# An H3 convolution and MLP stack on one core: a residual stream kept less its mean, and the second product's outputs in two 320-column banks

## The chip, the core and the metric

The kernel runs on one core of one Trainium2 chip. The metric is the device time of the whole kernel in microseconds, the median of three runs. The engines are TensorE (PE, matmuls; PEld, its weight loads), VectorE (DVE), ScalarE (ACT), GpSimd (POOL) and SyncE (SP, which issues nearly all transfers).

## The reference

Two identical layers act on a stream `x` of 2048 rows by 640 columns in float32. Each layer adds a convolution gated by the normalised stream and then a dense network:

```python
x = A_q
x = x + _A_ref(_layernorm(x, axis=-1), A_k, A_v, A_shift_k, A_ssm_k, A_ssm_D)
x = x + _B_ref(_layernorm(x, axis=-1), B_w1, B_w2)
x = x + _A_ref(_layernorm(x, axis=-1), A_k, A_v, A_shift_k, A_ssm_k, A_ssm_D)
x = x + _B_ref(_layernorm(x, axis=-1), B_w1, B_w2)
```

`_layernorm(x)` is `(x - m) / sqrt(v + 1e-5)` along the 640 columns. `_A_ref(q, k, v, ...)` computes `k_shift`, a causal convolution of `k` with 4 taps per column, multiplies it by `v`, convolves that along all 2048 rows with `ssm_k` (one filter per column, by FFT), adds `ssm_D` times the product, and returns `q * y`. The result `y` does not depend on `x`, so both layers use the same one. `_B_ref(x, w1, w2)` is `relu(x w1) w2`, with `w1` 640 by 1728 and `w2` 1728 by 640.

## The kernel before, in words

The 2048 rows are 8 chunks of two halves of 128 rows. `order` is the list of the dense network's passes ("mains"): chunks 0 and 1 go half by half through layer 0 and layer 1, then the chunks 2 to 7 both halves at once. Ahead of a chunk's first main, `conv_to` has its convolution worked out: `transform` (the short taps, the multiplication by `v`, cosine and sine transforms on TensorE) and `products` (a convolution over chunks in the transformed domain: multiplies and adds of 128x768 on VectorE, L559, L593, L596, L597, whose operands `Ax` and `Gx` are stored to memory and loaded back; then an inverse transform into `pq`, L619). The output is written as rows `ys` (L651, L652), stored as `Y` and loaded again as `y` before each layer's gate. For chunk 0 there is no store in between: `products` gates the stream itself (`direct`, L666, L667).

`prep` makes a main's input. `stats` computes the mean and the reciprocal deviation of each row: `negm` (L785, VectorE), a square with its sum (L788, ScalarE), a root, VectorE's reciprocal (L791), a few one-column refining steps on ScalarE (L796 to L800), and `xn`, the normalised stream (L810, ScalarE). The gate is `xn = y * xn` (L851) and `x = x + xn` with its row sums (L855), both on VectorE. Then `stats` runs once more and the result is split in a float16 high half (L884, ScalarE) and a low half (L885, VectorE), both transposed by transfers (L897). For the first halves the chain is another one (L840 to L869), and TensorE transposes the first of them (L904).

`main` multiplies with split weights: three matmuls for each product of high and low halves, but two where a low half is dropped. The first product (`mm1`, L1018 and L1020 in the first main, L1030 to L1033 in the others) goes to a bank `h` of up to 512 columns; ScalarE takes the relu as high half `hh` (L1086), VectorE the low half (L1087); the last group of 256 hidden columns has its own path (`tb`, `down`, `hb`, L1090 to L1101). The second product (`mm2`) has the hidden part as its stationary operand and writes 640 columns for each half:

```python
        o = lambda s, h: oc[:, s] if h else ob[s].t
        ds = (slice(0, H), slice(H, D)) if wino else (slice(0, 512), slice(512, D))
```

so the first 512 go to the bank `o0` or `o1` and the last 128 to a part of the bank `oc` (for the second main, of the bank `x`), which both halves share. The residual add (L1177) reads them in two instructions of 512 and 128 columns, with two partial sums that L1185 adds. The last three mains (`WINO`) use another scheme with 320-column banks (L957, with L1122 to L1143 behind it); this scheme's own arithmetic is the same before and after.

Weights are loaded once as float32. `norms` computes a power-of-two scale for each of the two weight matrices: TensorE multiplies each of the 28 weight tiles by itself into `pw` (L699), VectorE takes the diagonal's sum (`dg`, L704), TensorE adds over partitions (`pn`, L706), and a chain of one-column steps gives `wn`, `wnr`, `wpw` and `wsc` (L707 to L710). TensorE's 70 idle-time matmuls `spin` (L716) keep it running meanwhile. `wsplit` then splits each weight tile in a high half (L731, ScalarE) and a low half (L732, VectorE), of 128x640.

The order of every engine's instructions is written out by a planner. Each operation is given to it with an engine, a cost, what it reads and writes, and a priority (`CRIT`, `URGENT`, `SOON`, `FILL`, `BACK` and others). The planner simulates the engines by the costs, picks the best ready operation for each engine as it comes free, and starts an operation that opens a new buffer only when its ring has one. So a change in one operation's cost, buffer or priority can move others on any engine. The engines run their lists in order, waiting by semaphores.

Of the kernel before, what the change touches and what calls it, by code (L numbers as in the profile page):

```python
# [63 lines left out]
AADD, RADD = (), ()  # L64
# [11 lines left out]
class Tile:  # L76
    def __init__(self, ring, shape, dtype, name, stream=0):
        self.ring, self.shape, self.dtype, self.name, self.stream = ring, list(shape), dtype, name, stream
        self.t, self.left, self.writer, self.readers = None, 0, None, []
        if ring is not None:  # L80
            ring.lines.setdefault(stream, []).append(self)
# [4 lines left out]
    def r(self, pat, **kw):  # L86
        return self.t.rearrange(pat, **kw)

# [10 lines left out]
class Plan:  # L99
# [5 lines left out]
    def op(self, eng, cost, fn, reads=(), writes=(), prio=0, nbytes=0, late=0.0):  # L105
# [9 lines left out]
        for t in writes:  # L115
            if t.writer is not None:
                deps.add(t.writer)
            elif t.ring is not None and not t.left:
                o.new.append(t)
            deps.update(t.readers)  # L120
# [4 lines left out]
        o.tiles = list({id(t): t for t in (*reads, *writes)}.values())  # L125
# [8 lines left out]
    def order(self):  # L134
# [9 lines left out]
        def fits(o):  # L144
            at = {}
            for t in o.new:
                k = at.setdefault(t.ring, {})
# [14 lines left out]
        while n < len(self.ops):  # L162
# [27 lines left out]
            for e in engs:  # L190
# [17 lines left out]
                for t in best.new:  # L208
                    t.ring.free -= 1
                    t.ring.lines[t.stream].pop(0)  # L210
# [22 lines left out]
    def issue(self):  # L233
        out, end = self.order()
        for o in out:
            for t in o.new:
                t.t = t.ring.pool.tile(t.shape, t.dtype, tag=t.ring.tag, name=t.name, bufs=t.ring.bufs)
# [5 lines left out]
def tile_h3_mlp(ctx: ExitStack, tc: tile.TileContext, q, kT, vT, shk, hF, hR, dD, w1, w2, cM, cG, out):  # L243
# [65 lines left out]
    POOL.memset(c15.t, 1.5)  # L309
    shs = keep(const, [P, NDT, 4], "shs")  # L310
# [22 lines left out]
    def pieces(u, ap):  # L333
# [23 lines left out]
        "p0": (ps, "o0", 1, 1),  # L357
        "p1": (ps, "o1", 1, 1),
    }

    def transform(u):
        ring = ALT if u == [(0, 2), (0, 3)] else MAIN

        def R(k, shape, name):
            pl, tag, bufs, stream = ring[k]
# [184 lines left out]
    def products(u, at, gt, after):  # L550
# [98 lines left out]
        act(h, lambda: ACT.activation(qs.t, pq[:, 256 : 256 + h].rearrange("p (a b) -> p a b", a=n), AF.Copy), [pq], [qs], pr_)  # L649
        pp = lambda: pq[:, 0:h].rearrange("p (a b) -> p a b", a=n)  # L650
        dve(h, lambda: DVE.tensor_sub(yo(0), pp(), qs.t), [pq, qs], [dst[0]], pr_)  # L651
# [11 lines left out]
        if direct:  # L663
            xs, xns, sp0 = first[c]
            for s in range(2):
                dve(h, lambda s=s: DVE.tensor_mul(xns[s][:, cs], xns[s][:, cs], dst[s][:, cs]), [xns[s], dst[s]], [xns[s]], (CRIT, BACK)[s])  # L666
                dve(h, lambda s=s: DVE.scalar_tensor_tensor(xs[s][:, cs], xns[s][:, cs], 1.0, xs[s][:, cs], op0=ALU.mult, op1=ALU.add, accum_out=sp0[s][:, 0, t0 // 2 : t0 // 2 + 1]), [xns[s], xs[s]], [xs[s], sp0[s]], (CRIT, BACK)[s], 0.2)  # L667
# [14 lines left out]
    def norms():  # L682
        ones = T(cv, "u", 2, [P, P], "ones", stream=1)
        plan.op("POOL", 0.5, lambda: POOL.memset(ones.t, 1.0), [], [ones], SOON)
        out_ = []
        for k, e in ((0, 9), (1, 13)):
            pw2 = T(ps, *(("h", 2), ("oc", 1))[k], [P, 2, P], f"pw{k}", stream=1)
            for j in JS:
                for i in range(2):
# [5 lines left out]
                    def f(m=2 * j + i, t=t, pw2=pw2):  # L695
                        top = t.t.bitcast(BF16).rearrange("p (n two) -> p n two", two=2)[:, :, 1]
                        for d in range(NDT):
                            x = top[:, d * P : d * P + P]
                            PE.matmul(pw2[:, 0], x, x, start=(m == 0 and d == 0), stop=(m == 2 * JS[-1] + 1 and d == NDT - 1))  # L699
# [4 lines left out]
            dve(P, lambda jk=jk, pw2=pw2, s2=s2: DVE.scalar_tensor_tensor(jk.t, pw2[:, 0], 1.0, ident.t, op0=ALU.mult, op1=ALU.mult, accum_out=s2.t), [pw2, ident], [jk, s2], URGENT, 0.2)  # L704
            pn = T(ps, "x", 1, [P, 512], f"pn{k}", stream=1)
# [73 lines left out]
    def small(tag, name):  # L779
        return T(mlp, tag, 2, [P, 2], name)  # L780

    def stats(xs, sums, name, S, pr=0, fine=False):
        q_ = slice(S[0], S[-1] + 1)
        negm, ssq, sd, r, v, nmr = (small(k, k + name) for k in ("negm", "ssq", "std", "rstd", "var", "nmr"))
        dve(2, lambda: DVE.tensor_scalar(negm[:, q_], sums[:, q_], -1.0 / D, None, op0=ALU.mult), [sums], [negm], pr)  # L785
        for s in S:
# [13 lines left out]
            (0.19 * len(S), [r, negm], [nmr], lambda: [A(nmr[:, c], r[:, c], ident_, scale=negm[:, c]) for c in cols]),  # L800
        ]
        if fine:
            for cost, rd, wr, f in steps:
                act(0, f, rd, wr, pr, cost - 0.1)
        else:
            act(0, lambda: [f() for *_, f in steps], [ssq, sd, negm, heps, c15], [v, r, nmr], pr, sum(x[0] for x in steps))
# [20 lines left out]
    def add_sum(x, t, sums, s):  # L827
        plan.op("POOL", 1.1, lambda: POOL.dma_start(out=x.t, in_=t.t, accum_op=ALU.add), [x, t], [x], URGENT, 8 * D * P)
        if sums is not None:
            act(D, lambda: ACT.activation(t.t, x.t, AF.Copy, accum_out=sums[:, s : s + 1]), [x], [t, sums], URGENT, 0.1)  # L830

    def prep(a, layer, S, pr=0):
# [4 lines left out]
        if head:  # L837
            xs, _, sp0 = first[a]
# [3 lines left out]
        else:  # L842
# [6 lines left out]
            xns = stats(xs, sums, "A" + nm, S)  # L849
            for s in S:  # L850
                ew("ay", D, lambda e, s=s, xn=xns[s]: e.tensor_mul(xn.t, ys[s].t, xn.t), [ys[s], xns[s]], [xns[s]], URGENT)  # L851
                if (a, layer) in AADD:
                    add_sum(xs[s], xns[s], sums2, s)
                    continue
                dve(D, lambda s=s, xn=xns[s]: DVE.scalar_tensor_tensor(xs[s].t, xn.t, 1.0, xs[s].t, op0=ALU.mult, op1=ALU.add, accum_out=sums2[:, s : s + 1]), [xns[s], xs[s]], [xs[s], sums2], URGENT, 0.2)  # L855
# [24 lines left out]
        else:  # L880
            xns = stats(xs, sums2, "B" + nm, S, pr)
        for s in S if not head else ():
# [454 lines left out]
```

## Time and profile before

| what | before |
|---|---|
| runs | 858.65, 859.96, 864.69 us (median 859.96) |
| span of the profiled execution (no other time of it is given) | 858.4 us |
| instructions | 19,690 |
| TensorE matmuls busy | 843.4 us (98%) |
| VectorE busy | 743.1 us (87%) |
| ScalarE busy | 482.2 us (56%) |
| GpSimd busy | 46.5 us (5%) |
| transfers | 178.05 MB, mean 207 GB/s |

Busy time is an average over stages. The profile's page gives it for the whole span, the table by stretches for chosen windows; the list of waits names for each engine what it waited for, the groups of instructions show the mean time of one form, and the timeline shows each start. Matmuls overlap: a row of 0.38 us can be followed by the next after 0.22, so the spacing of starts says what a matmul costs.

### The profile page before, as it was taken

What the parts mean: (1) busy time and instruction counts of PE and PEld (TensorE: products, weight loads), DVE (VectorE), ACT (ScalarE), POOL (GpSimd) and SP (SyncE); (2) the same over time, 40 slices, a digit from 0 to 9 for tenths busy, and PEclk for the clock granted to TensorE, in tenths of its full rate; (3) what the DMA queues carried; (4) which work ended last, traced back from release to release, by engine and by line L of the source; (5) the groups of instructions that cost most, each with busy time, mean ns of one, the idle gap of its engine ahead of it and who ended that gap; (6) DMA issues with size and microseconds to landing.
All of it is one profiled execution on the core that took longest, in us unless ns stands there. A gap on an engine that the chain in (4) does not pass through costs nothing.

```text
span 858.4 us, 19690 instructions
## 1 busy us (share of the span) xinstructions
PE 843.4 (98%) x7808; PEld 663.1 (77%) x7808; DVE 743.1 (87%) x1367; ACT 482.2 (56%) x1121; POOL 46.5 (5%) x57
## 2 busy tenths in 40 slices
PE   8989999999999999999999999999999999999997
PEld 7867877777878777777777777878777777888886
DVE  7999999999889999999999999999897575645543
ACT  6597586455686375728448383835416275727331
POOL 2000000000011001101010000001000000000000
PEclk9999999999999999999999999999999999999999
DMA  9994968798999979889788988687985562110100
GB/s 325 391 296 150 270 192 287 213 340 281 310 260 284 325 192 270 201 255 252 197 245 243 223 236 168 184 189 241 266 272 200 135 216 31 44 20 2 43 20 32
DMA packets 133838, 178.05 MB, mean 207 GB/s; under 512 B 50545, under 2 KB 87153, under 8 KB 133746
## 3 DMA queue, kind: packets, MB, share of 16 engines
q1 hardware_dynamic: 125426, 166.31, 62.5%
q0 software_dynamic: 8320, 10.49, 8.1%
q8 instruction: 61, 1.00, 0.5%
q14 instruction: 31, 0.25, 0.1%
HBM read 122.03 MB, written 34.08 MB: 182 GB/s over the span
## 4 chain that ended last, share of the span: by engine, by line
PE 81%; DVE 10%; DMA 4%; ACT 3%; issue 2%; SPq 1%; DVEq 0%; ACTq 0%
PE h L1030 12%; PE h L1033 12%; PE h L1031 12%; PE o L1003 8%; PE o L1002 8%; PE o L1005 7%; PE o L957 7%; PE oc L1003 2%; PE oc L1002 2%; PE oc L1005 2%; DMA A<-at 1%; PE pq L619 1%; DVE pd L596 1%; PE hb L1030 1%; PE hb L1031 1%
## 5 line engine op out<-in xcount | busy, mean ns | idle before, releaser
L1030 PE MATMUL h<-xT,w 128*128 128x256 f16 (+1 forms) x1290 | 301.5, 252 | 0.7 <-DVE hh L1087 0.6
L1033 PE MATMUL h<-xT,w 128*128 128x256 f16 (+1 forms) x1290 | 301.3, 251 | 0.4 <-DVE w L732 0.4
L1031 PE MATMUL h<-xT,w 128*128 128x256 f16 (+1 forms) x1290 | 301.3, 251 | 0.0
L1031 PEld LDWEIGHTS <-w 128*128 128x128 f16 x1390 | 136.0, 98 | 11.2 <-issue 1.0
L1030 PEld LDWEIGHTS <-w 128*128 128x128 f16 x1390 | 135.9, 98 | 10.4 <-ACT w L737 0.2
L1003 PE MATMUL o<-w,hh 128*128 128x512 f16 x364 | 137.9, 379 | 0.4 <-DVE w L732 0.4
L1002 PE MATMUL o<-w,hh 128*128 128x512 f16 x364 | 138.1, 379 | 0.0
L1033 PEld LDWEIGHTS <-w 128*128 128x128 f16 x1290 | 126.2, 98 | 9.8 <-DVE w L732 0.6
L597 DVE TENSOR_TENSOR pacc<-pacc,pd 128x768 f32<-128x768 f32 x140 | 133.0, 950 | 0.5
L1003 PEld LDWEIGHTS <-hh 128*128 128x128 f16 x728 | 71.2, 98 | 45.8
L1002 PEld LDWEIGHTS <-hh 128*128 128x128 f16 x728 | 71.2, 98 | 44.6 <-issue 0.2
L1086 ACT ACTIVATE hh<-h 128x512 f16<-128x512 f32 (+1 forms) x103 | 50.4, 489 | 97.7 <-PE h L1033 94.4
L1005 PE MATMUL o<-w,hl 128*128 128x512 f16 x234 | 88.7, 379 | 0.0
L1003 PE MATMUL oc<-w,hh 128*128 128x128 f16 x364 | 79.7, 219 | 0.0
L1002 PE MATMUL oc<-w,hh 128*128 128x128 f16 x364 | 79.7, 219 | 0.0
L596 DVE TENSOR_TENSOR pd<-Ax,Gx 128x768 f32<-128x768 f32 x83 | 77.8, 951 | 0.9 <-DMA Gx<-G 0.8
L1005 PEld LDWEIGHTS <-hl 128*128 128x128 f16 x468 | 45.8, 98 | 27.6
L1005 PE MATMUL oc<-w,hl 128*128 128x128 f16 x234 | 51.2, 219 | 0.0
L394 ACT ACTIVATE tp<-kt,shs 128x256 f32<-128x256 f32 (+1 forms) x78 | 42.7, 574 | 13.0 <-DVE acc L431 10.8
L1087 DVE SCALAR_TENSOR_TENSOR hl<-h,hh 128x512 f16<-128x512 f32 x55 | 37.6, 685 | 11.0 <-ACT hh L1086 11.0
L596 DVE TENSOR_TENSOR pd<-at,Gx 128x768 f32<-128x768 f32 x46 | 43.2, 951 | 0.6 <-DMA Gx<-G 0.5
L412 POOL DMA_DIRECT2D gs<-hr x20 | 19.6, 980 | 387.5 <-DVE pacc L593 189.1
(232 smaller groups left out, 1666.6 us busy)
## 6 DMA issues: line engine op xcount, KB each, us to landing
Ax<-A SPq DMA_DIRECT2D x89, 384.0 KB, 4.5
Gx<-G SPq DMA_DIRECT2D x89, 384.0 KB, 4.1
G<-gt SPq DMA_DIRECT2D x30, 384.0 KB, 5.2
A<-at SPq DMA_DIRECT2D x30, 384.0 KB, 4.6
y<-Y SPq DMA_DIRECT2D x30, 320.0 KB, 4.7
ws<-in_w SPq DMA_DIRECT2D x28, 320.0 KB, 6.6
x<-in_q SPq DMA_DIRECT2D x16, 320.0 KB, 5.5
out_dram<-x SPq DMA_DIRECT2D x16, 320.0 KB, 4.0
```

Source lines behind the costliest of these rows:

```text
L394: ACT.activation(o[:, i : i + m], kview(i, m, j), AF.Copy, scale=shs[:, t, j : j + 1])
L596: ew(f"mac{j % POOLMOD}", 768, lambda e, pd=pd, av=av, gv=gv: e.tensor_mul(pd.t, av(), gv()), [ax, gx], [pd], pr_)
L597: dve(768, lambda i=i, pd=pd: DVE.tensor_add(acc[:, i], acc[:, i], pd.t), [acc, pd], [acc], pr_)
L957: PE.matmul(b[:, c : c + w], x, y[:, z : z + w], start=done[i] == 1, stop=done[i] == total[i])
L1002: PE.matmul(z, hh[:, c], wh[:, d], start=(j == JS[0] and i == 0 and (h == 0 or s == S[0])), stop=False)
L1003: PE.matmul(z, hh[:, c], wl[:, d], start=False, stop=end and tail)
L1005: PE.matmul(z, hl[:, c], wh[:, d], start=False, stop=end)
L1030: PE.matmul(p[:, z], wh, xv(t, 0), start=b, stop=False)
L1031: PE.matmul(p[:, z], wh, xv(t, 1), start=False, stop=tail and e)
L1033: PE.matmul(p[:, z], wl, xv(t, 0), start=False, stop=e)
L1086: act(2 * R, lambda p=p, hh=hh: ACT.activation(hh.t, p.t, AF.Relu), [p], [hh], URGENT)
L1087: dve(2 * R, lambda p=p, hh=hh, hl=hl: DVE.scalar_tensor_tensor(hl.t, p.t, 0.0, hh.t, op0=ALU.max, op1=ALU.subtract), [p, hh], [hl], URGENT)
```

## The change

*The gate.* Before, `x + y * ((x - m) r)` took one ScalarE and two VectorE instructions. After, ScalarE computes `q = 1 + r * y` and one VectorE instruction `x = (x - m) * q` with its row sums. This is the old result less `m`, so the stream is kept less its mean: `MEAN` holds the means of each half (`keepm`, one-column ScalarE steps), and in layer 1 ScalarE adds them back to `x` (16 instructions of 128x640). For chunk 0, `products` forms `q` from the two parts of `pq` directly, and the rows that are stored for the next layer (`qs`, `yd`) get the priority `BACK`.

*Negative means* (`negm` in `stats`) move from VectorE to ScalarE.

*The banks.* A second product's half has two banks of 320 columns (`banks`, tags `oA` and `oB`), and one VectorE instruction over both reads them for the residual add. The sums of `norms` (`pw1`, `pn`), the transposes of the first half and one of the transforms use the same banks. `o0`, `o1`, `oc` and `x` are gone, as is a path that was off (`AADD`, `RADD`).

The core of the diff:

```diff
-        dve(2, lambda: DVE.tensor_scalar(negm[:, q_], sums[:, q_], -1.0 / D, None, op0=ALU.mult), [sums], [negm], pr)
+        act(2, lambda: ACT.activation(negm[:, q_], sums[:, q_], AF.Copy, scale=-1.0 / D), [sums], [negm], pr, 0.1)
...
-            xns = stats(xs, sums, "A" + nm, S)
+            negm, r, _ = stats(xs, sums, "A" + nm, S, gate_=True)
             for s in S:
-                ew("ay", D, lambda e, s=s, xn=xns[s]: e.tensor_mul(xn.t, ys[s].t, xn.t), [ys[s], xns[s]], [xns[s]], URGENT)
...
-                dve(D, lambda s=s, xn=xns[s]: DVE.scalar_tensor_tensor(xs[s].t, xn.t, 1.0, xs[s].t, op0=ALU.mult, op1=ALU.add, accum_out=sums2[:, s : s + 1]), [xns[s], xs[s]], [xs[s], sums2], URGENT, 0.2)
+                qx = T(mlp, "xn", 2, [P, D], f"q{nm}{s}")
+                act(D, lambda s=s, qx=qx: ACT.activation(qx.t, ys[s].t, AF.Identity, scale=r[:, s : s + 1], bias=one.t), [ys[s], r, one], [qx], URGENT, 0.09)
+                dve(D, lambda s=s, qx=qx: DVE.scalar_tensor_tensor(xs[s].t, xs[s].t, negm[:, s : s + 1], qx.t, op0=ALU.add, op1=ALU.mult, accum_out=sums2[:, s : s + 1]), [qx, xs[s], negm], [xs[s], sums2], URGENT, 0.2)
+            keepm(a, negm, S)
...
             xns = stats(xs, sums2, "B" + nm, S, pr)
+            if layer:
+                for s in S:
+                    act(D, lambda s=s: ACT.activation(xs[s].t, xs[s].t, AF.Identity, bias=MEAN[a][:, s : s + 1]), [xs[s], MEAN[a]], [xs[s]], URGENT, 0.1)
...
+    def banks(tag, name, stream=0, shape=(512,), dtype=F32):
+        x = T(ps, tag, 1, [P, 2, *shape], name, dtype, stream)
+        return [Bank(x, k) for k in range(2)]
...
+        pw1, pn = banks("oB", "pw1", 2)
...
-            pn = T(ps, "x", 1, [P, 512], f"pn{k}", stream=1)
...
+        ob = {s: banks(("oA", "oB")[s], f"o{n}{s}") for s in S}
...
-        o = lambda s, h: oc[:, s] if h else ob[s].t
-        ds = (slice(0, H), slice(H, D)) if wino else (slice(0, 512), slice(512, D))
+        o = lambda s, h: ob[s][h][:, 0:H]
+        ds = (slice(0, H), slice(H, D))
...
-            for h in range(2):
-
-                def f(s=s, h=h):
-                    d = ds[h]
-                    acc = {"accum_out": sp[:, s, h : h + 1]} if layer == 0 else {}
-                    DVE.scalar_tensor_tensor(xs[s][:, d], o(s, h), fac[s].t, xs[s][:, d], op0=ALU.mult, op1=ALU.add, **acc)
-
-                dve(128 if h else 512, f, [oc if h else ob[s], fac[s], xs[s]], [xs[s]] + ([sp] if layer == 0 else []), URGENT, 0.15)
+
+            def f(s=s):
+                acc = {"accum_out": sums[:, s : s + 1]} if layer == 0 else {}
+                xv_ = xs[s].t.rearrange("p (h d) -> p h d", h=2)
+                DVE.scalar_tensor_tensor(xv_, ob[s][0].whole[:, :, 0:H], fac[s].t, xv_, op0=ALU.mult, op1=ALU.add, **acc)
+
+            dve(D, f, [*ob[s], fac[s], xs[s]], [xs[s]] + ([sums] if layer == 0 else []), URGENT, 0.15)
```

The planner gives other orders with this. Three places are shown. The first is VectorE's list in the head, where chunk 0's gate, the first weight norm (`dg`, `wn`, `wpw`, `wsc`) and the first halves' inputs (`xc`, `xl`) stand together. Before (rows of the list; a name ends in its buffer number):

```order
L707 TENSOR_SCALAR wn_195<-pn_691 128x1
L667 SCALAR_TENSOR_TENSOR x_1_291,sp_1_191<-xnA_01_503,x_1_291 128x256
L666 TENSOR_TENSOR xnA_00_496<-xnA_00_496,yd_531 128x128
L709 TENSOR_SCALAR wpw_197<-wnr_196 128x1
L652 TENSOR_TENSOR yd_579<-pq_4_619,qs_4_687 128x128
L667 SCALAR_TENSOR_TENSOR x_0_286,sp_0_190<-xnA_00_496,x_0_286 128x128
L710 TENSOR_SCALAR wsc_198<-wpw_197 128x1
```

After, at the row where the first half's `xc` is done and the first `dg` follows:

```order
L910 TENSOR_SCALAR xc_0_00_737<-x_0_296,negmB_0_0_731 128x640
L736 SCALAR_TENSOR_TENSOR dg_746,ws_196<-pw_486,ident 128x128
L912 RECIPROCAL rstdB_0_0_752<-stdB_0_0_750 128x1
L886 TENSOR_REDUCE sums_0_1_759<-sp_1_193 128x1
L551 TENSOR_TENSOR at_2_466<-at_2_466 128x2x256
L738 TENSOR_SCALAR wn_197<-pw_636 128x1
L736 SCALAR_TENSOR_TENSOR dg_777,ws_201<-pw_636,ident 128x128
L914 SCALAR_TENSOR_TENSOR xl_0_00_734<-xc_0_00_737,rstdB_0_0_752,xh_0_00_762 128x640
L740 TENSOR_SCALAR wpw_199<-wnr_198 128x1
L738 TENSOR_SCALAR wn_202<-pw_636 128x1
L908 TENSOR_SCALAR negmB_0_1_806<-sums_0_1_759 128x1
L741 TENSOR_SCALAR wsc_200<-wpw_199 128x1
```

The first scale `wsc` stood ahead of the first half's `xc`, between the gate's steps; now it stands behind `xc` and behind the second matrix's `dg`.

The second place is TensorE's list. Before, the matmul `pn` of the first norm stands between the norm matmuls of the weight tiles `ws_60` and `ws_61` of the first matrix:

```order
L699 LDWEIGHTS ws_60_571
L699 MATMUL pw_623<-ws_60_571 128x128
L706 MATMUL pn_691<-ws_194,ones 128x1
L699 LDWEIGHTS ws_61_585
L699 MATMUL pw_623<-ws_61_585 128x128
```

After, it stands behind the last of the 28 tiles, `ws_51`:

```order
L731 LDWEIGHTS ws_51_667
L731 MATMUL pw_636<-ws_51_667 128x128
L737 MATMUL pw_636<-ws_196,ones 128x1
L747 LDWEIGHTS ident_173
L747 MATMUL spin_766<-ident_173 128x128
```

A little later on TensorE, the second half's first product (it reads `xT_0_10`) begins at row 1098 of the list before, behind blocks of the first half's second product up to the tile `w_60`:

```order
L1005 LDWEIGHTS hh_6_1128
L1005 MATMUL oc_1046<-w_60_1258,hh_6_1128 128x128
L1030 LDWEIGHTS w_00_754
L1030 MATMUL h_0_1298<-xT_0_10_1140,w_00_754 128x128
L1031 LDWEIGHTS w_00_754
L1031 MATMUL h_0_1298<-xT_0_11_1183,w_00_754 128x128
```

After, it begins at row 842, behind the blocks of `w_00` and `w_01`:

```order
L1051 LDWEIGHTS hh_0_941
L1051 MATMUL o_1089<-w_01_1065,hh_0_941 128x320
L1076 LDWEIGHTS w_00_818
L1076 MATMUL h_0_1111<-xT_0_10_988,w_00_818 128x128
L1077 LDWEIGHTS w_00_818
L1077 MATMUL h_0_1111<-xT_0_11_1018,w_00_818 128x128
```

The first main's first product starts at row 574 in both, so 128 fewer matmuls now stand between the two starts.

The third place is SyncE's list around the load `Ax_1_0_2`, a convolution operand, near the chunk 0 main of layer 1. Before:

```order
L542 DMA A_1_83<-at_1_2890 128x768
L542 DMA A_2_84<-at_1_2890 128x768
L584 DMA Ax_1_0_2_2943<-A_2_74 128x768
L897 DMA_TRANSPOSE xT_0_00_2908<-xh_0_01_2864 128x5x128
L897 DMA_TRANSPOSE xT_0_01_2911<-xh_0_01_2864 128x5x128
```

After:

```order
L407 DMA kt_1_2896<-in_kT 128x2x262
L945 DMA_TRANSPOSE xT_0_00_2833<-xh_0_01_2812 128x5x128
L945 DMA_TRANSPOSE xT_0_01_2837<-xh_0_01_2812 128x5x128
L407 DMA vt_1_2928<-in_vT 128x2x256
L568 DMA G_3_125<-gt_3_2881 128x768
L568 DMA G_4_126<-gt_3_2881 128x768
L696 DMA Y_2_154<-ys_0_2930 128x128
L696 DMA Y_2_162<-ys_0_2930 128x128
L696 DMA Y_3_155<-ys_0_2930 128x128
L696 DMA Y_3_163<-ys_0_2930 128x128
L611 DMA Ax_1_0_2_3005<-A_2_74 128x768
```

The load went from row 147 to row 157 of this list, behind the loads of the next `kt` and `vt` and behind four `Y` stores that followed it before.

More of the change, by code (lines that the diff above doesn't have):

```diff
@@ L309, in tile_h3_mlp @@
     POOL.memset(c15.t, 1.5)
+    one = keep(const, [P, 1], "one")
+    POOL.memset(one.t, 1.0)
     shs = keep(const, [P, NDT, 4], "shs")
@@ L364, in R @@
         def R(k, shape, name):
+            if isinstance(ring[k], str):
+                return banks(ring[k], name, 1)[0]
             pl, tag, bufs, stream = ring[k]
```

134 lines of the change are left out of this document (74 added, 60 removed).

## The prediction

> **What bounds the kernel now.** I read the page first: busy time by engine, then the chain that ended last.
>
> ```profile
> PE 843.4 (98%) x7808; PEld 663.1 (77%) x7808; DVE 743.1 (87%) x1367; ACT 482.2 (56%) x1121; POOL 46.5 (5%) x57
> ...
> PE 81%; DVE 10%; DMA 4%; ACT 3%; issue 2%; SPq 1%; DVEq 0%; ACTq 0%
> ```
>
> TensorE is busy for 843.4 of 858.4 us, so work taken from VectorE is worth something only where TensorE waits for it. The table by stretches shows where that is (columns: stretch, length, busy time of PE, PEld, DVE, ACT and POOL with the instructions, granted clock, DMA share, GB/s).
>
> ```profile
> 42.00:76.00 34.00, 31.52 (x373) 24.05 (x374) 33.35 (x62) 30.23 (x58) 0.00 (x0) 1.00 0.69 223
> ...
> 140.00:180.00 40.00, 37.49 (x420) 30.16 (x418) 37.83 (x67) 20.99 (x53) 0.00 (x0) 1.00 0.85 271
> 180.00:300.00 120.00, 119.90 (x1303) 95.32 (x1301) 114.29 (x206) 73.06 (x182) 9.32 (x9) 1.00 0.99 295
> 300.00:500.00 200.00, 200.00 (x1656) 152.31 (x1655) 198.31 (x321) 117.56 (x269) 21.89 (x21) 1.00 0.84 230
> 500.00:660.00 160.00, 160.00 (x1326) 120.76 (x1324) 149.00 (x235) 78.72 (x185) 10.91 (x10) 1.00 0.80 223
> ```
>
> The reader is to see the second pair of numbers: from 180 to 660 TensorE is idle for 0.1 us in all, though VectorE is 93 to 99% busy; the granted clock is 1.00 everywhere. What can be won lies ahead of 42 us, in 42 to 76 (34.00 − 31.52 = 2.5 us idle) and in 140 to 180 (2.5 us). The end is fixed. The last matmul of the timeline is this one, ending at 853.1, and behind it come only the last main's residual add and its stores, which the change leaves alone.
>
> ```profile
> 852.79 0.30 PE L957 MATMUL o<-w,hl 128*128 128x320 f16 x1
> ```
>
> So 858.4 − 853.1 = 5.3 us stay, and everything that a lighter VectorE can return is under 10 us.
>
> **TensorE's own work.** The second product's outputs go from 512 + 128 columns to 320 + 320. These rows of the timeline (start, duration; a row that ends in x2 is two matmuls) show the spacing of starts:
>
> ```profile
> 100.33 0.38 PE L1002 MATMUL o<-w,hh 128*128 128x512 f16 x1
> ...
> 100.98 0.22 PE L1002 MATMUL oc<-w,hh 128*128 128x128 f16 x1
> ...
> 101.15 0.38 PE L1002 MATMUL o<-w,hh 128*128 128x512 f16 x1
> ...
> 734.74 0.43 PE L957 MATMUL o<-wt,gs 128*128 128x320 f16 x2
> ...
> 735.15 0.43 PE L957 MATMUL o<-wt,gs 128*128 128x320 f16 x2
> ```
>
> Three of 512 columns go from 100.33 to 100.98, 0.216 each; three of 128 from 100.98 to 101.15, 0.056 each; three of 320 from 734.74 to 735.15, 0.136 each. A pair was 0.272 and is 2 × 0.136 = 0.272: equal columns, equal count, no change. L1003 has as many as L1002, so the pairs number 2 × 364 + 234 + 104 = 1,066:
>
> ```profile
> L1002 PE MATMUL o<-w,hh 128*128 128x512 f16 x364 | 138.1, 379 | 0.0
> ...
> L1005 PE MATMUL o<-w,hl 128*128 128x512 f16 x234 | 88.7, 379 | 0.0
> ...
> L1005 PE MATMUL o<-w,hh 128*128 128x512 f16 x104 | 39.4, 379 | 0.9 <-DVE hh L1087 0.9
> ...
> L1002 PEld LDWEIGHTS <-hh 128*128 128x128 f16 x728 | 71.2, 98 | 44.6 <-issue 0.2
> ```
>
> Each pair has a weight load of 98 ns before a 128-column matmul, and yet these start 56 ns apart: the load does not set the pace. **Term: 0.** [...]
>
> **VectorE and ScalarE.**
>
> ```profile
> L851 DVE TENSOR_TENSOR xnA<-y,xnA 128x640 f32<-128x640 f32 x30 | 24.0, 820 | 3.4 <-ACT xnA L810 2.4 <-DMA y<-Y 0.9
> L1177 DVE SCALAR_TENSOR_TENSOR x<-o,winv,x 128x512 f32<-128x512 f32 x24 | 17.9, 745 | 2.4 <-PE o L1005 2.4
> L1177 DVE SCALAR_TENSOR_TENSOR x<-oc,winv,x 128x128 f32<-128x128 f32 x24 | 8.3, 345 | 2.3 <-PE oc L1005 2.3
> L785 DVE TENSOR_SCALAR negmB<-sums 128x2 f32<-128x2 f32 x13 | 2.2, 167 | 0.1
> L810 ACT ACTIVATE xnA<-x,nmrA,rstdA 128x640 f32<-128x640 f32 x32 | 28.0, 910 | 0.1
> ```
>
> VectorE loses the 30 multiplies of L851 (24.0 us); the one instruction that is left of each pair has the columns of the add that was there before (L855). The residual add becomes one of 640 columns for a pair of 1.09 us. No row shows a VectorE read across two banks; it lies between 0.82 (L851, as many columns) and 1.09 (the pair), and I take 0.82, the nearest row in shape: 0.27 × 26 = 7 us. Negative means leave, about 27 × 0.16 = 4 us. That is about 35 us by durations, some 28 once the overlap of about 0.08 between neighbours is taken off. ScalarE gets 16 restores of 128x640 (at most L810's 0.91 each, 14.6 us), 32 one-column means and the negative means, and makes fewer scaled means: about 18 us more, an estimate, on an engine that is idle for 376 of 858 us. The work that hides all this is TensorE's, without a gap from 180 on, so none of it is a term. If that cover is gone, each restore stands ahead of the next input's high half, and 16 of them cost up to 15 us; in the stretches above TensorE waited nowhere after 180 for an input to be ready, so I take 0.
>
> **The head, 0 to 76 us.** Here TensorE waits for weights to be split in two halves (L731, L732), which wait for the scale chain (L704 to L710).
>
> ```profile
> 34.27 0.33 PE L706 MATMUL pn<-ws,ones 128*128 128x1 f32 x2
> ...
> 38.45 0.45 PE L699 MATMUL pw<-ws 128*128 128x128 bf16 x5
> ...
> 42.29 0.22 PE L1018 MATMUL h<-xT,w 128*128 128x128 f16 x1
> ...
> 67.22 0.22 PE L1030 MATMUL h<-xT,w 128*128 128x128 f16 x1
> ```
>
> VectorE's rows at the same place:
>
> ```profile
> 35.82 0.15 DVE L710 TENSOR_SCALAR wsc<-wpw 128x1 int32<-128x1 int32 x1
> ...
> 39.23 0.87 DVE L732 SCALAR_TENSOR_TENSOR w<-ws,wsc,w 128x640 f16<-128x640 f32 x1
> ...
> 46.70 1.67 DVE L732 SCALAR_TENSOR_TENSOR w<-ws,wsc,w 128x640 f16<-128x640 f32 x2
> ```
>
> Before, the first norm's `pn` runs at 34.27 and its scale is ready at 35.97, 1.7 later. In the changed order `pn` stands behind all 28 weights' norm matmuls, the last of which started at 38.45 when its weight had landed: `pn` at about 38.75, the scale at 40.5. ScalarE's first high half then ends near 41.5, and VectorE's first low half starts near 42.0 (39.23 before), the second near 42.8, ending at 43.65. So the first product starts **1.35 later**. The two splits that begin at 46.70 are w_30 and w_31, over at 48.3; in the changed order eight splits of 0.8, two filter loads' adds, the second half's low half and some short rows stand from 42.0 on, so they are over near 51.9.
>
> Against that, the second half's input comes sooner. Before, its first matmul stands at 67.22, and from 42.29 to there 24.93 us went by for what ahead of it is 206 matmuls × 0.056, nine blocks of six (0.82 each) and 0.9 of convolution: 19.8 us of work, 5.2 lost. The list of TensorE's waits in 42 to 76 names part of them, on relu halves and on splits (us in total, times, longest):
>
> ```profile
> PE h L1030 <- DVE hh L1087: 0.6, 1, 0.6
> PE hb L1099 <- ACT tb L1090: 0.6, 1, 0.6
> ...
> PE o L1003 <- DVE w L732: 0.4, 2, 0.2
> ```
>
> After, only 9.2 us of work stand between the two starts (128 fewer matmuls), so from about 55 TensorE has two halves to draw on. Then the waits for splits are paid only up to there: w_31 at 51.9, the product that needs it (1.7) and two blocks (1.6) done at 55.15, where 9.2 us of work took 11.5; 2.3 us lost, nothing much after. 1.35 + 2.3 against 5.2 is −1.5; I take **−1.0**, because half a microsecond of further split waits is likely. Ends: −3 (the splits catch up) and +2 (they go on starving TensorE until 75).
>
> **140 to 180 us.**
>
> ```profile
> PE pg L471 <- ACT at L521: 1.2, 1, 1.2
> ...
> 172.50 0.51 ACT L394 ACTIVATE acc<-kt,shs 128x256 f32<-128x256 f32 x1 [4.38 <-DMA kt<-in_kT]
> ```
>
> The 1.2 us come from ScalarE standing 4.38 us at kt, with the copies that TensorE needs queued behind. The changed SP order asks for kt ahead of Ax_1_0_2, so that wait should shrink; but Ax_1_0_2 goes ten rows back, behind two loads, two G stores and four Y stores. Before, it was issued and used so:
>
> ```profile
> 160.02 0.49 SPq L584 DMA_DIRECT2D Ax<-A  x1
> ...
> 170.08 0.95 DVE L593 TENSOR_TENSOR pacc<-Ax,gt 128x768 f32<-128x768 f32 x1
> 170.95 0.42 DVE L1087 SCALAR_TENSOR_TENSOR hh<-h,hh 128x256 f16<-128x256 f32 x1
> ```
>
> Moved bytes of kt, vt, 2 G and Y, 262 + 256 + 2 × 384 + 4 × 64 KB, at 271 GB/s are 5.8 us; with the queue it lands around 173 instead of 164, 2 to 3 us after its old use. VectorE stands in front of L1087 then, unless it has other rows ahead. I take **−0.5**, with ends −2.5 (all waits go) and +4.
>
> **Sum.** Against the profiled execution's span, −1.0 (head), −0.5 (140 to 180) and 0 (TensorE's columns, the end): 858.4 − 1.5 = 856.9. The median of the runs shown, 859.96, is 1.56 above the span before; the same on top gives 858.5.
>
> **Rivals.** A kernel's 1%, 8.6 us, is about what a measurement here tells from no change.
> - *Starved by transfers.* With 28 us less of VectorE work its convolution steps run ahead of the loads in 180 to 300, where the DMA share is 0.99. An Ax or Gx that is late by the 2 to 3 us worked out above stops VectorE with a relu's low half behind it, and TensorE then stops once its own next product is done. At 2.5 us in each of about five mains it is +12: 870. It decides from the point where the load lands after the low half is due. For it: the 0.99 and the 4.38; against it: VectorE is busy for 114 of these 120 us before, so its loads hardly ever came late, and the bytes are the same.
> - *Late weights.* The 3.6 us by which w_31 is late are paid in full and the second half doesn't fill: +4, 862.
> - *Weight loads set the pace.* By the 98 ns of the rows, the pair falls from 98 + 216 to 272: 42 × 1,066 = 45 us, 814. The 56 ns starts all but exclude it.
> - *Less VectorE work pays.* All waits of 42 to 180 go and the head gains its 3 us: −8, 850.
>
> **How the numbers follow.** Forecast (854.5 to 866) 0.65; starved 0.20, of which 0.17 beyond 1% (868.6); late weights 0.06; restores uncovered 0.03 (up to 873); less work pays 0.05, of which 0.04 beyond 1% (851.4); weight loads 0.01. So faster 0.05; slower 0.17 + 0.03 = 0.20; the same 0.75. The forecast's own ends are 858.5 − 2 − 2 and 858.5 + 3 + 4.5, 854.5 and 866; the range is drawn out below, half way to the rival that pays, and above to 869, just short of the starved 870: about 0.05 is left out below, 0.15 above.
>
> **What would show it.** In the changed profile: 320-column starts 0.136 apart; VectorE near 715 us, ScalarE near 500; first product at 43 to 44; the second half's first product near 55; the scale chain after 40; PE's idle time in 180 to 660 still near 0. TensorE waiting on the relu's low half while VectorE waits for Ax or Gx would show the starved case; a matmul spacing of 98 ns or more would show the weight loads. Wrong I would be if TensorE idles anywhere after 180.

## The result and the profile after

| | before | after |
|---|---|---|
| median of 20 runs each | 860.85 us (858.65 to 864.69) | 859.55 us (857.09 to 862.29) |
| ratio, 95% interval | 1 | 0.998 (0.9971 to 0.999) |
| span of the profiled execution | 858.4 us | 857.4 us |
| VectorE busy | 743.1 us | 717.8 us |
| ScalarE busy | 482.2 us | 497.1 us |
| TensorE matmuls busy | 843.4 us | 842.9 us |

The changed kernel is 0.2% faster, a real difference and a fifth of the 1% that the chances called no change. VectorE lost 25.3 us of work; the time lost 1.3 (medians) or 1.0 (spans). These are the page's lines of the changed kernel, busy time and chain:

```profile
PE 842.9 (98%) x7808; PEld 707.2 (82%) x7808; DVE 717.8 (84%) x1253; ACT 497.1 (58%) x1177; POOL 47.2 (6%) x58
...
PE 75%; DVE 12%; DMA 7%; ACT 3%; issue 2%; SPq 0%; DVEq 0%; ACTq 0%
```

and its table by stretches, with the columns as before (the second pair of numbers is TensorE's):

```profile
42.00:76.00 34.00, 33.11 (x403) 28.23 (x401) 33.59 (x56) 33.19 (x64) 0.00 (x0) 1.00 0.71 224
...
140.00:180.00 40.00, 39.52 (x432) 33.96 (x430) 38.48 (x66) 20.62 (x51) 0.00 (x0) 1.00 0.92 285
180.00:300.00 120.00, 119.24 (x1299) 101.69 (x1298) 107.38 (x182) 79.58 (x201) 10.34 (x10) 1.00 0.98 285
300.00:500.00 200.00, 198.97 (x1647) 165.38 (x1645) 196.76 (x296) 116.64 (x272) 21.01 (x20) 1.00 0.88 234
500.00:660.00 160.00, 160.00 (x1325) 131.53 (x1324) 145.71 (x212) 82.44 (x200) 10.76 (x10) 1.00 0.82 222
```

TensorE's idle time fell from 2.5 to 0.9 us in 42 to 76 and from 2.5 to 0.5 in 140 to 180, and rose from 0.1 to 1.8 in 180 to 500. So part of what the early stages gave was lost again later, though VectorE has less to do.

Windows at fixed times compare different work, since the orders differ. The next table, worked out from the starts of all matmuls, doesn't have that fault. Every matmul is counted at its usual spacing, the median of its kind over all kernels. Float32 matmuls are taken by operands too, since those of 256 columns start 0.216 us apart for some operands and 0.12 for others. For the matmul ahead of which stands so much TensorE work, the table gives its start less that work, which is the time that TensorE has lost by then. Where a number stays equal down a column, nothing is lost. The columns behind "after" belong to the runs below.

```
work ahead  before  after  mul out  512+128  +24 us  +48 us  negm alone  +24 planned
    45 us     10.2   11.2     10.6     11.3    12.8    11.1        11.0         11.0
    60        12.4   11.2     12.9     11.4    12.9    11.1        13.4         10.9
   100        12.9   11.8     13.4     12.4    14.2    13.3        13.8         12.3
   140        13.9   13.4     13.8     14.3    20.0    22.9        16.9         16.8
   160        16.6   13.6     16.6     14.5    20.1    23.0        17.9         16.9
   200        17.3   15.2     17.2     16.4    21.7    25.7        18.3         17.3
   300        17.8   15.7     17.7     17.1    24.1    32.4        18.9         20.3
   400        18.0   15.9     17.8     18.0    26.5    39.3        19.0         20.4
   460        18.1   17.5     17.9     19.0    28.4    42.9        19.4         20.6
   480        18.1   17.5     18.0     19.1    28.4    42.9        31.6         25.6
   600        18.5   17.6     18.3     19.6    29.6    48.1        31.9         25.7
   800        18.7   17.6     18.4     19.7    31.0    57.8        31.9         25.7

work ahead  gate alone  banks alone  negm undone  norm early  before, +3 ns  after, +3 ns
   100 us         12.8         12.9         13.2        12.7           11.9          12.5
   160            13.6         14.5         15.4        16.7           13.4          17.1
   200            15.5         15.0         16.2        18.7           13.9          17.2
   300            16.8         15.6         16.6        19.1           22.0          18.4
   460            17.2         15.8         16.8        19.3           22.6          18.9
   480            17.2         19.7         17.8        19.4           22.6          19.1
   800            17.5         20.6         18.0        19.4           23.7          19.2
```

After against before: 1.1 us won by 100, 3.0 by 160, 2.1 by 300, most of that lost again between 400 and 460, and 1.1 left at the end.

### The profile page after: what moved, and what is told of

Read it like the earlier page. It is cut to its first block, busy times and chain, and to the rows that moved or that the text cites. A ratio compares the mean times of both kernels' runs of the same rounds, so it can differ in the third digit from the quotient of the medians.

```text
span 857.4 us, 19663 instructions
## 1 busy us (share of the span) xinstructions
PE 842.9 (98%) x7808; PEld 707.2 (82%) x7808; DVE 717.8 (84%) x1253; ACT 497.1 (58%) x1177; POOL 47.2 (6%) x58
## 4 chain that ended last, share of the span: by engine, by line
PE 75%; DVE 12%; DMA 7%; ACT 3%; issue 2%; SPq 0%; DVEq 0%; ACTq 0%
PE h L1076 11%; PE h L1077 11%; PE h L1079 11%; PE o L1049 9%; PE o L1048 9%; PE o L1051 9%; PE o L1003 7%; DMA ws<-in_w 2%; DVE pd L623 2%; DVE pacc L624 2%; DMA hf<-in_hF 1%; DVE pacc L620 1%; PE hb L1076 1%; PE hb L1077 1%; DMA y<-Y 1%
## 5 line engine op out<-in xcount | busy, mean ns | idle before, releaser
L1049 PE MATMUL o<-w,hh 128*128 128x320 f16 x728 | 216.7, 299 | 0.4 <-DVE w L763 0.4
L1048 PE MATMUL o<-w,hh 128*128 128x320 f16 x728 | 216.9, 299 | 0.0
L1051 PE MATMUL o<-w,hl 128*128 128x320 f16 x468 | 139.9, 299 | 0.2 <-DVE hl L1133 0.2
L1051 PE MATMUL o<-w,hh 128*128 128x320 f16 x208 | 62.2, 299 | 1.0 <-DVE hh L1133 0.6
L458 DVE TENSOR_TENSOR acc<-acc,tp 128x512 f32<-128x512 f32 (+1 forms) x54 | 36.1, 669 | 1.4 <-ACT tp L421 1.2
L620 DVE TENSOR_TENSOR pacc<-Ax,gt 128x768 f32<-128x768 f32 x35 | 33.3, 950 | 1.5 <-DMA Ax<-A 1.5
```

The lines of the kernel that those rows point to most:

```text
L620: dve(768, lambda i=i, av=av, gv=gv: DVE.tensor_mul(acc[:, i], av(), gv()), [ax, gx], [acc], pr_)
L1048: PE.matmul(z, hh[:, c], wh[:, d], start=(j == JS[0] and i == 0), stop=False)
L1049: PE.matmul(z, hh[:, c], wl[:, d], start=False, stop=end and tail)
L1051: PE.matmul(z, hl[:, c], wh[:, d], start=False, stop=end)
```

## Experiments

Two theories stood at the start of the runs. *The order*: what changed the time is where the waits fall in the new order lists, and VectorE's load as such is covered by TensorE. *The load*: the lighter VectorE is what was paid out. The lists of a kernel stay word for word the same if an instruction is made longer or shorter and the planner isn't told, so the load can be changed without the order, and the order without the load.

### The load put back: 24 and 48 us more on VectorE at the changed kernel's order

```diff
-                dve(D, lambda ...: DVE.scalar_tensor_tensor(xs[s].t, ...), ..., URGENT, 0.2)
+                dve(D, lambda ...: (DVE.scalar_tensor_tensor(xs[s].t, ...), DVE.tensor_mul(qx.t, qx.t, qx.t)), ..., URGENT, 0.2)
```

The second kernel has `tensor_mul` twice.

> The changed kernel with one extra 128x640 multiply behind each of the 30 gates on VectorE (on a scratch tile; the order lists of all engines are those of the changed kernel, since the planner's costs are untouched): VectorE gets its 24 us back. Theory 1, the places of the waits in the order lists made the difference and VectorE's load itself is covered by TensorE: 859 to 861, at most 1.5 us above the changed kernel. Theory 2, the 25 us lighter VectorE is what was paid out: back to the time before, 861 or above, by 2 us or more.

> As the run with 24 us, but two extra multiplies, 48 us in all: VectorE at about 765 us, more than before the change. Theory 1: still little, 860 to 863, until VectorE falls behind in the stretch from 300 to 500 us, where it is 98% busy. Theory 2: twice the step of the run with 24 us, 863 to 866.

Measured: 871.75 us, ratio to before 1.0127 (1.0099 to 1.0155), and 898.74 us, 1.0444 (1.0423 to 1.0466). Against the changed kernel that is 12.2 and 39.2 us. The load theory said "861 or above" for the first, and it is 11 us above the time before; for the second both theories had it far too small. VectorE is busy for 740.8 us in the first, less than the 743.1 of the kernel before, and yet 10.9 us are lost against that kernel. TensorE's longest groups of waits in the kernel with 24 us (us in total, times, longest):

```profile
PE hb L1145 <- ACT tb L1136: 4.5, 6, 1.3
PE hb L1076 <- DVE hh L1133: 3.7, 3, 2.2
```

The same two groups in the changed kernel:

```profile
PE hb L1076 <- DVE hh L1133: 0.5, 1, 0.5
...
PE hb L1145 <- ACT tb L1136: 0.3, 1, 0.3
```

The waits for VectorE grew with its load, and so did those for ScalarE, whose busy time is the same (497.5 us): ScalarE itself waits 21.5 us for the gate's instructions (L899), against 12.0 in the changed kernel. In the profiled execution TensorE is not busy for 23.0 us, 8.5 more than in the changed kernel, and its granted clock is 0.96 in 0 to 42 us and 0.83 in 150 to 160, which costs some 3.4 more (0.04 × 42 + 0.17 × 10; the last section shows how). The other part of the loss is not the clock: two of the four runs have the mean clock 0.998 and take 869.5 and 870.8 us. The loss isn't in one place: against the changed kernel the table has 6.6 us of it by 140 and 13.4 by 800. With 48 us the second 24 cost 27 us, more than their own time. So the cover of VectorE's work was thin in one direction: these lists have no room for 23 us more, though VectorE is idle for 140 of the changed kernel's 857. The extra multiply always stands in the gate, on the way to the next input; what the same time costs elsewhere on VectorE was not tried.

### The load taken away at the order before

```diff
-                ew("ay", D, lambda e, s=s, xn=xns[s]: e.tensor_mul(xn.t, ys[s].t, xn.t), ...)
+                ew("ay", D, lambda e, s=s, xn=xns[s]: e.tensor_mul(xn[:, 0:1], ys[s][:, 0:1], xn[:, 0:1]), ...)
```

> The kernel before with the gate's multiply cut to one column (it leaves out the multiplication by y in 639 of 640 columns for the 30 gates ahead of the later halves); all order lists are those of before. VectorE is 22 us lighter at the same order. Theory 1: only waits that name VectorE can shrink, 0 to 1 us faster, 859.8 to 860.9. Theory 2: the whole gain without any change of order, 858.5 to 859.3.

Measured: 859.84 us, ratio 0.9979 (0.9963 to 0.9995). VectorE's busy time fell by 17 us, not 22, to 726.0. By its median the run is at the edge of theory 1 (859.8), by its ratio it has the gain of the whole change, as theory 2 said, because the kernel before took 861.1 beside it; the trace (column "mul out") shows 0.3 us won at the end. So this run doesn't tell the theories apart. It does show that 17 us less at the same lists is worth 0.05 to 0.4%, where 23 us more at the other lists cost 1.5%.

### The same load with lists that know of it

```diff
-                dve(D, lambda ...: (DVE.scalar_tensor_tensor(...), DVE.tensor_mul(...)), ..., URGENT, 0.2)
+                dve(D, lambda ...: (DVE.scalar_tensor_tensor(...), DVE.tensor_mul(...)), ..., URGENT, 0.94)
```

> The changed kernel with the same extra multiply behind each of the 30 gates as in the run that took 871.8, but the planner is told its cost (0.74 us more for the gate), so that it writes the orders for the heavier VectorE. VectorE's load is the same, about 741 us. Theory A, the 12 us came from order lists that were written for a lighter VectorE (the kernel before has 743 us of VectorE work and no such loss): 859 to 863. Theory B, in the changed kernel's form VectorE's load itself has become the bound: 868 to 874 again.

Measured: 867.29 us, ratio 1.008 (1.0061 to 1.01). The lists written for the load win back 4.5 of the 12.2 us, and neither theory's number was met. Until 460 of the table this kernel has lost 20.6, against 28.4 without the planner's knowledge and 17.5 in the changed kernel; 5.0 more are lost in one place behind that, where an input's transposes came late. The timeline of TensorE there:

```profile
489.06 0.28 PE L1076 MATMUL h<-xT,w 128*128 128x256 f16 x1 [2.54 <-DMA xT<-xh]
489.78 0.35 PE L1077 MATMUL h<-xT,w 128*128 128x256 f16 x1 [0.44 <-DMA xT<-xh]
489.93 0.42 PE L1079 MATMUL h<-xT,w 128*128 128x256 f16 x1
490.14 0.42 PE L1076 MATMUL h<-xT,w 128*128 128x256 f16 x1
...
493.31 0.27 PE L1076 MATMUL h<-xT,w 128*128 128x256 f16 x1
493.42 0.27 PE L1077 MATMUL h<-xT,w 128*128 128x256 f16 x1
```

The waits are 3.0 us; behind them matmuls start 0.21 apart for some 3.4 us instead of 0.11 (the granted clock is 0.61 in 489 to 493), which costs 1.7 more (the last section comes back to it).

So a good third of what the unforeseen load costs is a matter of the order, and by 460 of the table it is 7.8 of 10.9 us; of this kernel's remainder, 5.0 are one place. How the rest divides between load and order is not shown.

### The order changed, the load not

Both kernels got other lists by a planner's cost that is 3 ns higher for each VectorE operation. No instruction differs.

```diff
-        plan.op("DVE", base + n / 960.0, fn, reads, writes, prio)
+        plan.op("DVE", base + 0.003 + n / 960.0, fn, reads, writes, prio)
```

> The kernel before with no instruction changed; the planner's cost of every VectorE operation is 3 ns higher (0.067 to 0.073 for its fixed part), which gives other orders on all engines. Theory A, the place of the waits in the orders is worth as much as the change itself: the time moves by 1 to 10 us either way, more likely up. Theory B, the orders are worth less than the change: 860 to 862.

> The changed kernel with no instruction changed and the planner's cost of every VectorE operation 3 ns higher. Theory A: 860 to 870, the gain of 0.2% gone or more. Theory B: 858.5 to 860.5, the gain stays whatever the order.

Measured: the kernel before 865.55 us, ratio 1.006 (1.0039 to 1.0081), 4.5 us slower than itself; the changed kernel 860.93 us, 0.9993 (0.998 to 1.0005), level with the kernel before. Theory A fits both. For the kernel before, the order alone is worth three times the change: its other lists are 3.4 us ahead of the old ones by 200 of the table and lose 8.1 between 200 and 300. For the changed kernel, other lists with the same instructions give back 0.13 of its 0.2%.

### The parts of the change

The gate alone (the mean kept and added back; 512 + 128 columns and VectorE's negative means as before):

```diff
-            xns = stats(xs, sums, "A" + nm, S)
+            negm, r, _ = stats(xs, sums, "A" + nm, S, gate_=True)
...
-                ew("ay", D, lambda e, s=s, xn=xns[s]: e.tensor_mul(xn.t, ys[s].t, xn.t), ...)
+                act(D, lambda s=s, qx=qx: ACT.activation(qx.t, ys[s].t, AF.Identity, scale=r[:, s : s + 1], bias=one.t), ...)
```

> The kernel before with the gate alone (one VectorE instruction, the mean kept and added back), negative means on VectorE and 512 + 128 columns as before. The planner gives a head as in the changed kernel (second half's first product at row 842). Theory 1 (the order): most of the head's gain, 858.5 to 860.5. Theory 2 (VectorE's load, 24 of 25 us lighter): the whole gain, 859.1 (ratio 0.998).

Measured: 858.47 us, ratio 0.9977 (0.9956 to 0.9999), the whole gain. But it wasn't won in the head, as theory 1 had it: by 100 of the table this kernel has lost 12.8, as much as the kernel before (12.9; the changed kernel 11.8), though its second half's first product stands at the changed kernel's row. It won 3.0 by 160 and kept 1.2. The same total came from other places.

The banks alone:

```diff
-            ob = {s: T(ps, f"o{s}", 1, [P, 512], f"o{n}{s}") for s in S}
+        ob = {s: banks(("oA", "oB")[s], f"o{n}{s}") for s in S}
...
```

> The kernel before with the two 320-column banks alone: one residual add for two, 7 us less on VectorE; the head's order is as before (second half's first product at row 1098). Equal column work and no gain in the head: 859.5 to 861.5, ratio 0.999 to 1.001. If the column form costs or saves TensorE time, 10 us or more away.

Measured: 862.3 us, ratio 1.0011 (0.9998 to 1.0024): no gain, within its interval. The table tells more: until 460 this kernel is 2.3 us ahead of the kernel before (15.8 against 18.1), and then it loses 3.9 in one place, where an input's transposes came late again (waits of 1.6 and 0.3 us, and a granted clock of 0.57 in the 4 us behind them).

The columns alone, at the changed kernel's order:

```diff
-        o = lambda s, h: ob[s][h][:, 0:H]
-        ds = (slice(0, H), slice(H, D))
+        o = lambda s, h: ob[s][h][:, 0 : 128 if h else 512]
+        ds = (slice(0, H), slice(H, D)) if wino else (slice(0, 512), slice(512, D))
...
```

> The changed kernel with the second product's outputs in 512 + 128 columns of the same two banks, and the residual add in two instructions again (with the sum of two partial sums); the order lists are unchanged. By equal column work (0.216 + 0.056 against 2 x 0.136): TensorE's time the same, 859 to 860.5, the 7 us on VectorE being covered. If the 320-column form saves TensorE time by its weight loads: 10 us or more slower.

Measured: 861.12 us, ratio 1.0005 (0.9992 to 1.0018), 1.6 us above the changed kernel. No tens of microseconds: the weight loads set no pace. VectorE is busy for 723.0 us, 5.2 more, and at the half microsecond lost for each microsecond in the run with 24 us that would be 2.8. The expected 860.5 at most was missed by a little: at these lists, taking the two banks back undoes the whole gain, whether by VectorE's 5.2 us or by the form itself.

The negative means alone, and undone:

```diff
-        dve(2, lambda: DVE.tensor_scalar(negm[:, q_], sums[:, q_], -1.0 / D, None, op0=ALU.mult), [sums], [negm], pr)
+        act(2, lambda: ACT.activation(negm[:, q_], sums[:, q_], AF.Copy, scale=-1.0 / D), [sums], [negm], pr, 0.1)
```

> The kernel before with the negative means on ScalarE alone, 4 us less on VectorE. Its head has another order too: the second half's first product at row 918. Theory 1: 859.5 to 861, moved by the order alone. Theory 2: a sixth of the gain, 860.6.

Measured: 873.62 us, ratio 1.0151 (1.0115 to 1.0186), 12.5 us slower where 0 was expected. The timeline of TensorE has it in one place, a first product that waits for its transposed input:

```profile
493.70 0.40 PE L1030 MATMUL h<-xT,w 128*128 128x256 f16 x1 [7.86 <-DMA xT<-xh]
496.15 0.40 PE L1031 MATMUL h<-xT,w 128*128 128x256 f16 x1 [2.06 <-DMA xT<-xh]
```

Between 460 and 480 of the table this kernel loses 12.2 us, these waits and the slower start behind them (the granted clock is 0.50 in 493 to 497 and 0.68 in 497 to 500). VectorE made the low halves of that input from 484.5 on, where it did from 471.8 in the kernel before, and SyncE issued the last transpose at 491.99, behind two stores and two loads. It is the same place in the work where the run with the planned load lost 5.0 and the banks alone 3.9. Then the same part was taken out of the changed kernel (the diff above, backwards):

> The changed kernel with the negative means back on VectorE (4 us more there, other orders). If the 12 us that this part cost alone lie in ScalarE's price for it: faster than the changed kernel by several us, 850 to 856. If they lay in that one order, where the transposes of an input came 8 us late: 858 to 862, the same as the changed kernel within 3 us.

Measured: 860.14 us, ratio 0.9989 (0.9976 to 1.0003), the same as the changed kernel within 1 us. So, as far as two runs with different lists can show it, ScalarE's price for the negative means isn't what cost 12.5 us; one order of the lists was.

### The head: the first norm early again

```diff
-            jk = T(cv, "qs", 1, [P, P], f"dg{k}", stream=1)
+            jk = T(mlp, "hl", NH, [P, P], f"dg{k}")
```

> The changed kernel with a buffer of its own for the diagonal of the weight norms, so that the first norm's matmul over partitions goes back ahead of the other weights' (TensorE row 320 of the list instead of 411) and the first scale is ready some 5 us sooner; the second half's first product goes back to row 1002 from 842. Theory 1 with the head's account (first product 1.35 earlier, but waits for splits return): 858 to 861. If the late norm costs its whole lateness: 3 us faster, 856.5.

Measured: 860.47 us, ratio 0.9998 (0.9989 to 1.0008), 0.9 us above the changed kernel. The first scale was ready at 35.57 instead of 40.45, the first product began at 42.59 instead of 43.51, and nothing was won: by 100 of the table this kernel has lost 12.7, as the kernel before. So the lateness of the norm isn't a cost that waits to be collected. The rest of the lists changed too, and most of its later loss (16.7 against 13.6 by 160) belongs to them.

## Why the prediction was right, point by point

It gave 858.5 (852.5 to 869.0) and no change by 1%; measured were 859.55 and 0.2%. For the span, it gave 856.9 and 857.4 was measured. Most of the 1.05 us between the medians is the starting point: it stood on three runs of the kernel before with a median of 859.96, and twenty give 860.85. What was right is the main argument, that 25 us of VectorE's work lie behind TensorE's and some 1 us is paid. That the sum came so near is partly luck. Its terms were −1.0, −0.5 and 0; by the table they were −1.1 (to 100), −1.9 (100 to 160) and +1.9 (from there on), two misses that nearly cancel.

**TensorE's columns, 0.** Right. The timeline of the changed kernel has 320-column starts 0.136 apart (three from 100.29 to 100.70):

```profile
100.29 0.30 PE L1048 MATMUL o<-w,hh 128*128 128x320 f16 x1
100.43 0.30 PE L1049 MATMUL o<-w,hh 128*128 128x320 f16 x1
100.56 0.30 PE L1051 MATMUL o<-w,hh 128*128 128x320 f16 x1
100.70 0.30 PE L1048 MATMUL o<-w,hh 128*128 128x320 f16 x1
```

The rival of the weight loads is out. The end is unchanged as well, 857.4 − 852.0 = 5.4 after the last matmul:

```profile
851.74 0.30 PE L1003 MATMUL o<-w,hl 128*128 128x320 f16 x1
```

**The head, −1.0.** Right in size and in its steps. Rows of TensorE and VectorE in the changed kernel:

```profile
38.66 0.33 PE L737 MATMUL pw<-ws,ones 128*128 128x1 f32 x2
43.51 0.22 PE L1064 MATMUL h<-xT,w 128*128 128x128 f16 x1
55.42 0.22 PE L1076 MATMUL h<-xT,w 128*128 128x128 f16 x1
```

```profile
40.31 0.14 DVE L741 TENSOR_SCALAR wsc<-wpw 128x1 int32<-128x1 int32 x1
...
50.48 1.67 DVE L763 SCALAR_TENSOR_TENSOR w<-ws,wsc,w 128x640 f16<-128x640 f32 x2
```

The late `pn` is at 38.66 (38.75 worked out), the scale ready at 40.45 (40.5), the first product at 43.51 (43.65), w_31 over at 52.15 (51.9), the second half's first product at 55.42 (55.15). By 100 us of work the gain is 1.1. Between 45 and 60 of the table the kernel before loses 2.2 us and this one nothing, which fits the second half's earlier input. That this input is enough isn't shown: the gate alone has it as early and had won nothing by 100.

**140 to 180, −0.5.** Right in sign, and kt was asked for earlier (156.55, 166.70 before), so that ScalarE's wait for it is gone. But the size is wrong: TensorE's idle time fell by 2.0 us here, near the end of −2.5 that the prediction gave if all waits went. The step on Ax_1_0_2 had its landing 4 us too late. Its timeline:

```profile
164.50 0.85 SPq L611 DMA_DIRECT2D Ax<-A  x2
...
169.03 0.96 DVE L620 TENSOR_TENSOR pacc<-Ax,gt 128x768 f32<-128x768 f32 x1 [1.45 <-DMA Ax<-A]
169.91 0.42 DVE L1133 SCALAR_TENSOR_TENSOR hh<-h,hh 128x256 f16<-128x256 f32 x1
```

It was issued 4.5 us later than before and landed near 169, not 173, since the rows ahead of it were issued earlier too. VectorE stood at it for 1.45 us with the relu's low half behind, as foreseen; TensorE didn't wait for it.

**From 180 on, 0.** This is the step that failed: "TensorE's, without a gap from 180 on, so none of it is a term". The prediction's own sign of being wrong was "if TensorE idles anywhere after 180", and it came: 1.8 us idle in 180 to 500. Between 400 and 460 of the table 1.6 us were lost, of which these three waits at TensorE name 1.04:

```profile
439.36 0.31 PE L1051 MATMUL o<-w,hl 128*128 128x320 f16 x1 [0.24 <-DVE hl L1133]
...
454.01 0.66 PE L521 MATMUL pt<-ident,sd 128*128 128x128 f32 x4 [0.45 <-ACT ob L502]
...
467.34 0.27 PE L1145 MATMUL hb<-tb,down 128*128 128x256 f16 x1 [0.35 <-ACT tb L1136]
```

The term took over, for new lists, what the profile of the old ones showed. No row of a profile in which TensorE never waits says how much later an engine may be before it does. The runs with more work showed how little room there is: 23 us more cost 12.

**VectorE and ScalarE** came to 717.8 and 497.1 us (715 and 500 forecast). The residual add over two banks, for which 0.82 was taken between 0.82 and 1.09, took 0.877:

```profile
L1211 DVE SCALAR_TENSOR_TENSOR x<-o,winv,x 128x640 f32<-128x640 f32 x24 | 21.0, 877 | 5.6 <-PE o L1051 5.6
```

**The rivals.** Late weights and weight loads are out. So are uncovered restores: none of the listed waits of TensorE after 180 is for an input, and no restore stands on ScalarE ahead of the two waits that name it. Less work pays is out as it stood (850), and what little was paid can't be told from the order. The starved case, +12, didn't come in this kernel. A loss of its size came in the run of the negative means alone, by another way: an input's transposes were late, and TensorE's waits there name no Ax or Gx.

What stays open is whether the 0.2% comes from the lighter VectorE or from the luck of the lists. The runs bound each part (17 us less at equal lists: 0.05 to 0.4%; other lists at equal load: 0.1 to 0.6%), and these overlap.

## What to carry to other kernels

In a kernel that is 98% TensorE, sum what TensorE waits for, stage by stage, before counting what a lighter VectorE saves: 25 us became 1. That cover is one-sided: check the other direction too. Here the lists lost half a microsecond, and then a whole one, for each microsecond that an operation took longer than the planner thought. Look also for a place where many orders lose: in four of the fourteen kernels here one place, the input's transposes between 460 and 480 us of work, cost 1 to 12 us. And where a planner writes the order, rewrite it once or twice with a cost moved by nothing before trusting a difference below 1%: here 3 ns moved one kernel by 4.5 us.

## What the runs showed of the hardware that was not expected

Some waits of a few microseconds cost TensorE more than their length here. In the run with 24 us more, the longest wait is 2.2 us and ends at 154.35; the table by stretches has a granted clock of 0.83 there, and 1.00 on both sides. In the banks alone, waits of 1.6 and 0.3 us end at 483.85, and the clock is 0.57 for the next 4 us:

```profile
150.00:160.00 10.00, 7.80 (x56) 6.01 (x55) 8.98 (x17) 6.24 (x18) 0.00 (x0) 0.83 0.80 243
```

```profile
484.00:488.00 4.00, 4.00 (x23) 2.96 (x22) 4.00 (x7) 1.54 (x3) 0.00 (x0) 0.57 0.65 252
```

By those shares each is 1.7 us more, beside the waits (0.17 × 10 and 0.43 × 4), as much as half the clock for 3.4 us. In the kernel with the planned load the same shows by single matmuls, 0.21 apart and then 0.11 again 3.4 us later (489.93 to 493.31). But the length of the wait didn't decide it. In the run with 48 us more, a wait of 2.63 us left the clock at 1.00:

```profile
691.54 0.27 PE L1076 MATMUL hb<-xT,w 128*128 128x256 f16 x1 [2.63 <-DVE hl L1133]
```

```profile
685.00:695.00 10.00, 7.37 (x60) 5.69 (x59) 9.79 (x17) 5.47 (x17) 0.00 (x0) 1.00 0.00 0
```

The waits of the changed kernel in the stretches shown (0.6 us at most) leave no such trace: its granted clock is 1.00 in all of them. What takes the clock down isn't shown: idle times of 2.2 us and of 1.6 + 0.3 us came before it, and one of 2.63 us came without it. So far as these runs go, the loss was steeper than the waits: these lists first lose short waits, then long ones and sometimes clock.

The weight loads' busy time rose by 44 us, from 663.1 to 707.2, with equal loads and unchanged time. Before, a load of 98 ns in front of matmuls that start 56 ns apart overlaps its neighbour (loads of 0.10 us start at 100.98, 101.04 and 101.09), and busy time counts that stretch once: summed by groups, the loads take 808 us in both kernels. At 136 ns they no longer overlap (100.29, 100.43 and 100.56). For 1,066 pairs at 98 − 56 = 42 ns that is 45 us. The run with 512 + 128 columns, with the same lists as the changed kernel, is back at 662.5.
